# Six PSUM tiles of one bank for the products of a Strassen-like expert layer, new planner costs and a new order of work

## The chip, the core and the metric

The kernel runs as one program on one core of a Trainium2 chip. The core has five engines that run side by side, each with its own queue that is worked off strictly in order: TensorE (PE, matrix products; its weight loads are listed as PEld), VectorE (DVE), ScalarE (ACT), GpSimd (POOL) and SyncE (SP, which issues most of the DMAs). Products are summed up in PSUM, which has eight banks of 512 float32 numbers per partition. The metric is the device time of one execution in microseconds (us); lower is better.

## The reference

What is computed is an attention block whose output goes through a layer of experts. Each of 2304 tokens picks 2 of 8 experts by noisy logits; an expert is two matrix products with a ReLU between them.

```python
# attention: q, k, v are (4, 8, 576, 64)
q_rot, k_rot = rotate(q), rotate(k)
attn = softmax(q_rot @ k_rot.T / sqrt(64))
x = (attn @ v).transpose(0, 2, 1, 3).reshape(2304, 512)
# experts: w1 is (8, 512, 1024), w2 is (8, 1024, 512)
noisy = x @ w_gate + log1p(exp(x @ w_noise)) * noise
top2, top2_w = two largest of noisy per token, softmax over the two
for e in range(8):
    for k in range(2):
        mask = top2[:, k] == e
        h = maximum(x[mask] @ w1[e], 0)
        out[mask] += top2_w[mask, k, None] * (h @ w2[e])
```

## The kernel before, in words

**Two halves.** Attention and routing fill roughly the first 345 us. The tokens are written to a table in memory with room for 624 (`CAP`) tokens per expert (five tiles of 128), and the experts follow. Every float32 operand is split into a float16 high and a float16 low part, and each product is the sum of three: high by high, high by low, low by high. ACT makes the high part of a piece and DVE the low part; the pair of instructions is called a cast here.

**Experts 0 and 1** are computed plainly. `up` makes one block of 128 hidden rows for 256 or 368 tokens at a time (12 matmuls for the narrow form, each 256 or 368 columns wide), into a PSUM tile from a ring of three (`big`, two banks each); ACT (L1559) and DVE (L1557) then write its high and low part to `hid`, and only then is the tile free for the third block after it. There are 16 blocks for the first 256 tokens of both experts and 16 wide ones (368 columns) for the rest.

**Experts 2 to 7** use seven products of half-size blocks in place of eight, for the first layer (`seven`). The 624 tokens are two halves of 312, and the 1024 hidden rows are taken in two passes `p`, each with two blocks of 128 rows, `g` = 0 and 1. Sums of weight blocks are made by DVE (L1303 to L1309, cast in L1291 and L1295) and sums of token blocks by POOL (`plan_turns`, L1354 to L1366, cast in L1370 and L1374). For each `p` the products run in the order P2, P1, P7, P6, P4, P5, P3, each for g = 0 and then g = 1, six matmuls of 312 columns at a time. They are added up in three PSUM tiles, called c, a and b, of two banks each: bank 0 of a tile belongs to g = 0, bank 1 to g = 1. Partial sums that are needed twice are copied to SBUF by ACT (`keep`, L1450: k1 after P1, k7 after P7, k2 after P6), added again by DVE (`join`, L1454: j11, j21, j22), and the finished quarters of the hidden layer go through ReLU to `hid` (`hide`, L1443 on ACT and L1441 on DVE): quarter 11 from c, 21 from b, 12 from a, and 22 from the copies in SBUF. Quarters 11 and 21 are read for both g in one instruction of 2 x 312 columns.

**Second layer.** `down` adds 24 matmuls of 512 columns into a tile of one bank (`dn`, a ring of two, called a down tile here); ACT scales it (`y`, L1634) and POOL adds its rows into the output (`spread`, L1643).

**What sets the order.** Each step is entered in a plan (`Plan.add`) with an engine, a duration, the steps it depends on and the buffers that it uses. `Plan.order` runs through the plan in simulated time and always starts the ready step of lowest priority number; the numbers in `CFG["dp"]`, one for each step, are added to the priorities. The order in which the steps are started is the order in which instructions are recorded for the engines, and it is fixed from then on. At run time an instruction waits through semaphores for the instructions that it depends on, as they are found from the tiles read and written, whatever the plan thought of their time.

Of the kernel before, what the change touches and what calls it, by code (L numbers as in the profile page):

```python
# [11 lines left out]
F32 = mybir.dt.float32  # L12
# [124 lines left out]
-20 2935 3206 -1718 -2012 -889 2833 4404 813 -264 2775 -2091 3378 2520 -4200 -555 -59 3739 1239 -2425 1328 1857 541  # L137
1731 -994 378 -3900 3008 -1979 -4553 -8 -3221 328 -3171 -921 -816 -284 242 1068 974 -2451 -82 5813 -913 4682 1180 5502
450 -543 5177 1264 936 -7 4727 -2533 -1839 -56 -760 785 -612 201 -5606 2097 -1110 238 -4268 -2037 2004 315 1567 -528
5925 6561 -2693 2544 2495 6494 358 -890 1789 -5127 -1907 -6509 -930 2280 5751 182 281 2260 113 223 1663 1222 473 1956  # L140
-365 89 1384 -417 724 1974 3373 1695 -625 1015 -2456 378 -1435 -871 -1680 869 1345 2982 2910 -1823 -589 -282 -258
-1914 6672 -552 219 1369 -3333 -1232 -1554 -1533 433 -1426 5310 -255 -3444 2150 -450 497 7553 -3948 521 -556 2815
-4797 -1994 -793 -6025 -1393 2002 -687 2569 2441 -1802 4019 -102 5322 509 2546 -3466 -2707 -7485 4070 4585 7698 -1354
-4162 -6438 -3748 4554 -3147 3530 -5284 -5734 -79 -19 -5230 -2269 1762 -53 -2801 -2692 -3814 -1054 -4707 -5370 -2335
3505 -655 2289 -4886 -5778 -1651 8257 4590 -378 -1056 -3623 -1022 -3014 -1981 -3423 -1771 -3914 -4682 -5788 -3312
-1153 -2329 -5816 -352 -223 -1365 -345 2932 427 -3068 -582 -4025 -2535 -3748 -3399 -459 -1075 4383 409 2227 -848 -3669
5340 -116 711 -4565 -675 -5589 -8881 3198 -1797 964 -1008 3759 4607 1097 -2978 4367 -3493 517 -3983 2305 -2224 -956
-1166 318 12 1142 -1124 -3789 1000 -1055 -721 -2210 1771 -4136 1674 -1397 4956 -4176 -2022 -5262 -241 -5058 -6736
-1466 -1994 -3337 7334 -1092 -3646 -1784 -3296 1951 1419 2833 -3878 2373 4868 -8596 -567 -3922 -4552 -5075 797 8989
1521 5332 -836 15 1950 -2365 570 -3691 6597 -2034 -2379 1096 1521 2348 2756 2911 -1633 -54 2741 572 2650 -143 3107  # L150
-2132 989 675 -1461 -1125 -938 2322 -2330 446 -730 1427 -382 5808 -383 2478 -3307 -584 -514 244 546 365 -1138 -457
-1372 585 1203 1935 -2118 -505 -920 1547 1164 2577 3085 -3523 211 2713 1097 544 443 -527 -1831 971 -996 -167 1178 774
-1828 -3308 465 -1014 1242 -265 648 -3251 -210 -4359 -261 119 -3433 1404 -386 -1274 1400 -688 -2361 -1871 899 334 -719
-2542 -190 -340 -106 2497 803 -2006 1602 -1626 3772 631 26 158 -1600 -163 388 -2908 1324 -720 -1070 -607 -2443 295 313
902 2122 1652 -728 854 3213 -48 -737 -1898 1253 1276 -4328 640 2949 359 2667 2111 1808 2082 -1925 -427 -78 594 -2373
1834 267 -3015 -28 1233 -715 -1145 -2563 854 -2598 -1427 648 -1543 -1512 100 2308 -428 -330 -77 814 -162 -1171 2632
-3574 -791 1090 1519 -599 2349 639 -331 -540 2479 -1094 781 1653 2217 -2051 1008 250 357 829 -1702 -2453 685 1253 1426
1432 501 3575 4393 732 -2277 1345 -3405 -1987 946 1503 -3280 -1832 228 755 -334 2032 -1447 1648 862 759 909 21 -660
2838 2983 -495 470 2516 1177 -1130 -2956 151 986 -953 790 -2830 -826 1394 900 -395 1140 -787 -966 2382 4866 3434 -401
-598 -3176 1813 1453 -1127 -1193 -1650 -2271 -1503 296 2068 1291 -425 3759 -762 2649 675 807 -1079 -2599 -1816 1949  # L160
-4331 -450 -8 606 280 -519 -1564 -245 1707 -1434 -694 -749 578 663 374 640 -1041 922 -1141 -1802 -3330 -1008 -3773
-4744 -1154 -1524 1241 2212 2762 518 387 -2497 1464 635 -901 -2389 -1214 193 264 2647 -1357 227 -124 152 -2548 400
-2834 2721 -1291 1761 -235 -2002 -680 331 963 -57 1228 -14 -2481 -1216 -1043 304 2443 -4481 969 3036 2635 -1831 -1182
786 737 -3898 -1866 -3171 5090 -1390 416 89 -1897 -157 1875 1019 -1283 320 1149 -2490 1000 360 271 1068 -177 1754 2189
3976 -131 946 2000 -147 105 -3204 -2409 1026 -1540 1659 4616 291 -253 -955 -515 -3285 1284 -961 -2554 -2372 2401 -73
-3263 -910 -1325 1421 -1479 -2403 -3694 447 -669 1293 -2539 -196 -814 1651 1733 -1978 549 1025 3513 387 382 1037 -1508
-131 2169 -187 1221 -891 -1190 2149 1664 -346 -1248 569 14 156 508 1495 968 -1635 2063 3392 824 -2278 465 -850 -3234
642 -1202 1127 725 427 -2014 569 -764 739 5699 -555 2525 -520 1634 -483 3036 2228 -3023 864 2778 -566 1534 -625 -3059
3206 3154 -768 -2052 1644 535 -1343 492 4811 -2844 2570 -4654 -556 -3476 1593 -1389 -1849 -1590 679 2786 767 1269
-1981 -3289 1351 -493 -3567 -238 -799 -2346 -3957 -25 791 -3086 1442 -998 -1576 1241 978 344 -97 -9 2488 43 -1323 4897  # L170
# [1738 lines left out]
```

## Time and profile before

| | us |
|---|---|
| median of 3 runs | 763.6 |
| lowest and highest | 760.75, 763.7 |
| profiled execution | 769.25 |
| its span (first instruction to last) | 767.5 |
| PE busy in the span | 709.8 |
| DVE, POOL, ACT busy in the span | 512.2, 421.2, 365.1 |

The profiled execution is a single one, and longer than the median of the others; what lies around its span is the difference of 1.75 us. Times of instructions below are counted from the span's start. A busy PE in this table is one that has a matmul under way. A wait is told by the engine that waits and by the instruction whose end released it. The page also gives PE's granted clock, in shares of full speed (2.4 GHz; the other level is 1.2 GHz).

### The profile page before, as it was taken

The numbers are of one execution on the slowest core, as the hardware profiler recorded it, in microseconds if no ns is written. First come the engines' busy times: TensorE is split into PE (matmuls) and PEld (weight loads), VectorE is DVE, ScalarE is ACT, GpSimd is POOL, SyncE is SP. The second block draws the span as 40 slices with busy tenths as digits, with TensorE's granted clock in tenths as the row PEclk, the third lists the DMA queues.
The fourth block names the chain that finished last, engine by engine and source line by source line (L and its number), as shares of the span: only waits on it lengthen the run. The fifth ranks groups of instructions, "written<-read, shape, count | busy, mean of one in ns | idle before, by whom it ended". The sixth has DMA issues, their size and how long they took to land.

```text
span 767.5 us, 18738 instructions
## 1 busy us (share of the span) xinstructions
PE 709.8 (92%) x7988; PEld 488.3 (64%) x7988; DVE 512.2 (67%) x801; ACT 365.1 (48%) x602; POOL 421.2 (55%) x332
## 2 busy tenths in 40 slices
PE   4899998899889899889999798999999999999996
PEld 4677777788777777778555345556465565554652
DVE  5757769886859669577217658929879497594331
ACT  2543555564546664855124236637456455473310
POOL 5699798896614686835611486191460822902311
PEclk9999999999799999999999999999999999999998
DMA  6686465966517594574674462663735627514211
GB/s 157 149 138 136 115 141 116 191 139 144 115 52 159 190 212 149 162 195 169 215 201 113 97 192 34 143 187 76 207 86 126 174 56 201 137 61 97 54 66 41
DMA packets 178285, 103.50 MB, mean 135 GB/s; under 512 B 150136, under 2 KB 154744, under 8 KB 178192
## 3 DMA queue, kind: packets, MB, share of 16 engines
q1 hardware_dynamic: 161632, 72.72, 40.2%
q0 software_dynamic: 8592, 20.38, 11.4%
q10 hardware_dynamic: 7968, 9.12, 3.6%
q8 instruction: 64, 1.05, 0.6%
q14 instruction: 29, 0.24, 0.1%
HBM read 49.92 MB, written 29.22 MB: 103 GB/s over the span
## 4 chain that ended last, share of the span: by engine, by line
PE 61%; DVE 11%; ACT 7%; issue 2%; DMA 1%; SPq 0%; POOL 0%; POOLq 0%; ACTq 0%; DVEq 0%
PE ps L574 27%; PE dn L574 26%; PE acc L574 7%; DVE nm L599 1%; DVE xr L813 1%; ACT p L699 1%; DVE w1l L1295 1%; DVE hid L1441 1%; DMA qt<-tq 1%; ACT xr L815 1%; ACT ps L699 1%; ACT xr L1450 1%; ACT hid L1443 1%; ACT w1h L1291 1%; DVE w2l L1178 1%
## 5 line engine op out<-in xcount | busy, mean ns | idle before, releaser
L574 PE MATMUL dn<-w2h,hid 128*128 128x512 f16 x640 | 193.9, 380 | 0.0
L1643 POOL DMA_INDIRECT out_dram<-y,meta x40 | 67.2, 1679 | 219.2 <-ACT y L1634 186.1
L574 PEld LDWEIGHTS <-hid 128*128 128x128 f16 x960 | 94.1, 98 | 111.1 <-issue 1.3
L574 PE MATMUL dn<-w2l,hid 128*128 128x512 f16 x320 | 121.6, 380 | 0.0
L710 POOL TENSOR_TENSOR p<-p 128x1152 f16<-128x1152 f32 (+1 forms) x48 | 100.0, 2096 | 29.9 <-ACT p L699 28.2
L699 ACT ACTIVATE p<-ps,pbias 128x576 f32<-128x576 f32 x112 | 79.9, 740 | 71.7 <-PE ps L574 70.3
L599 DVE TENSOR_REDUCE nm<-ps 128x2 f32<-128x576 f32 x128 | 90.6, 749 | 25.2 <-PE ps L574 24.9
L574 PE MATMUL ps<-qt,kt 64*128 64x288 f16 (+5 forms) x1200 | 85.4, 264 | 8.7 <-DVE nm L599 3.3
L574 PE MATMUL acc<-vb,p 128*128 128x65 f16 (+3 forms) x2040 | 78.4, 194 | 8.3 <-DVE xr L813 6.9
L574 PE MATMUL ps<-xt,w1h 128*128 128x312 f16 (+2 forms) x384 | 81.0, 304 | 4.8 <-DVE hid L1557 4.0
L574 PEld LDWEIGHTS <-p 128*128 128x128 bf16 (+3 forms) x2040 | 70.7, 98 | 21.0 <-issue 16.0
L574 PEld LDWEIGHTS <-w1h 128*128 128x128 f16 x640 | 62.8, 98 | 33.1 <-issue 9.4
L574 PE MATMUL ps<-kt,qt 64*128 64x288 f16 (+1 forms) x960 | 79.8, 291 | 2.9 <-DVE nm L599 0.8
L574 PEld LDWEIGHTS <-kt 64*128 64x128 f16 (+1 forms) x1200 | 54.2, 98 | 22.8 <-issue 14.6
L1634 ACT ACTIVATE y<-dn,gsc 128x512 f32<-128x512 f32 x33 | 22.6, 685 | 88.0 <-PE dn L574 74.2
L1178 DVE SCALAR_TENSOR_TENSOR w2l<-wst,w2h 128x1024 f16<-128x1024 f32 x25 | 41.4, 1671 | 29.8 <-ACT w2h L1176 29.8
L574 PEld LDWEIGHTS <-qt 64*128 64x128 f16 (+1 forms) x960 | 46.3, 98 | 19.0 <-issue 8.7
L574 PE MATMUL ps<-xt,w1l 128*128 128x312 f16 (+2 forms) x192 | 58.3, 303 | 0.0
L1441 DVE SCALAR_TENSOR_TENSOR hid<-ps,hid 128x624 f16<-128x624 f32 (+1 forms) x48 | 30.5, 639 | 32.6 <-ACT hid L1443 32.2
L1110 POOL DMA_INDIRECT xs_rows<-xr,r_ii x36 | 37.5, 1042 | 22.8 <-DVE gsc L1514 12.9
L574 PE MATMUL ps<-qlm,cm 64*128 64x288 f16 (+5 forms) x440 | 47.0, 255 | 0.0
L1450 ACT COPY xr<-ps 128x312 f32<-128x312 f32 x72 | 28.1, 423 | 28.1 <-PE ps L574 27.6
(196 smaller groups left out, 1289.8 us busy)
## 6 DMA issues: line engine op xcount, KB each, us to landing
wst<-in_moe_w_dram SPq DMA_DIRECT2D x51, 512.0 KB, 4.0
wst_r<-in_moe_w_dram SPq DMA_DIRECT2D x13, 512.0 KB, 6.0
out_dram<-pad ACTq DMA_DIRECT2D x18, 256.0 KB, 3.7
xs_rows<-pad ACTq DMA_DIRECT2D x8, 522.0 KB, 4.5
qin<-in_q_dram SPq DMA_DIRECT2D x16, 256.0 KB, 4.6
qin<-in_k_dram SPq DMA_DIRECT2D x16, 256.0 KB, 4.0
vin<-in_v_dram SPq DMA_DIRECT2D x16, 256.0 KB, 3.4
out_dram<-y,meta POOLq DMA_INDIRECT x40, 4.9
```

Source lines behind the costliest of these rows:

```text
L574: nc.tensor.matmul(o, w, m, start=first, stop=last, skip_group_check=True)
L599: nc.vector.tensor_reduce(nm()[:, u, :, h], x, axis=AX.X, op=OP.max, negate=True)
L699: nc.scalar.activation(x if way[u] == "P" else halves(whole(u), u, h), x, AF.Exp, bias=pbias, scale=0.125 / (QS * QS))
L710: E.tensor_tensor(b, whole(u), a, op=OP.subtract)
L813: nc.vector.tensor_tensor(at_, xx, to, op=OP.subtract)
L815: nc.scalar.copy(to, xx)
L1110: i = nc.gpsimd.indirect_dma_start(out=xs, out_offset=bass.IndirectOffsetOnAxis(ap=h["ii"][:, t, a:a + 1], axis=0), in_=r[:, slot(t)], in_ ...
L1178: nc.vector.scalar_tensor_tensor(lo[:, c:c + step], h[c], sc, hi[:, c:c + step], op0=OP.mult, op1=OP.subtract)
L1441: nc.vector.scalar_tensor_tensor(s["hl"][:, f0:f0 + n, cols:cols + HALF], src_(), 0.0, h, op0=OP.max, op1=OP.subtract)
L1450: add((nm, e, p, g), "ACT", .33, lambda: nc.scalar.copy(snap(k, g), bank(r, g)), deps=[dep], uses=[b[r, g], sb[k, g]], prio=pr)
L1634: nc.scalar.activation(y, dn(), AF.Copy, scale=s["gsc"][j])
L1643: i = nc.gpsimd.indirect_dma_start(out=out, out_offset=bass.IndirectOffsetOnAxis(ap=ids(e, j, 0), axis=0), in_=yt[0], in_offset=None, boun ...
```

## The change

1. **PSUM tiles.** Where experts 2 to 7 begin (`banks`), the ring of three two-bank tiles is closed, and a pool of six tiles of one bank each takes its place, one for each of c, a, b and each g. So that this can be done, the accumulator of the attention (`sml`) and the down tiles (`acc`) are placed from the other side of PSUM. The instructions that hide quarters 11 and 21 are split in two, one for each g; the plan has 48 steps more (2654, before 2606).
2. **Costs in the plan.** Sums of tokens on POOL are planned longer, loads of an expert's tokens get another issue time and a landing time by size, and a scatter on POOL is planned with 1.7 in place of 1.07.
3. **Order.** The table `CFG["dp"]` has new numbers from the routing of the third batch on; all steps before that keep theirs.

```diff
-20 2935 3206 -1718 -2012 -889 2833 4404 813 -264 2775 -2091 3378 2520 -4200 -555 -59 3739 1239 -2425 1328 1857 541
+-20 2935 3206 -1718 -2012 -889 2833 4404 813 -264 2775 -2588 4328 2216 -2425 -1857 1073 4370 2214 -2985 943 4208 454
...
-    big = ctx.enter_context(tc.tile_pool(name="big", bufs=3, space=PSUM))
-    manual, attn, early, sums_ = ExitStack(), ExitStack(), ExitStack(), ExitStack()
+    manual, attn, early, sums_, big_ = ExitStack(), ExitStack(), ExitStack(), ExitStack(), ExitStack()
+    big = big_.enter_context(tc.tile_pool(name="big", bufs=3, space=PSUM))
-    sml = sums_.enter_context(tc.tile_pool(name="sml", bufs=1, space=PSUM))
+    sml = sums_.enter_context(tc.tile_pool(name="sml", bufs=1, space=PSUM, side="right"))
...
-        pools["acc"] = ctx.enter_context(tc.tile_pool(name="acc", bufs=2, space=PSUM, reuse_waits="tile"))
+        pools["acc"] = ctx.enter_context(tc.tile_pool(name="acc", bufs=2, space=PSUM, side="right", reuse_waits="tile"))
...
-                return .08 + m * HALF * (1.04e-3 if E == "DVE" else 2.1e-3 if m == 4 else 2.6e-3)
+                return .08 + m * HALF * (1.04e-3 if E == "DVE" else 2.3e-3 if m == 4 else 3.1e-3)
...
-    zb = []
+    zb = {}
     def banks():
-        zb.extend(big.tile([128, 1024], F32, name="ps") for _ in range(3))
+        big_.close()
+        pz = ctx.enter_context(tc.tile_pool(name="zs", bufs=1, space=PSUM, reuse_waits="tile"))
+        for a in range(3):
+            for g in range(2):
+                zb[a, g] = pz.tile([128, 512], F32, name="z%d%d" % (a, g))
...
-            return zb[role[r]][:, 512 * g:512 * g + HALF]
+            return zb[role[r], g][:, 0:HALF]
...
-        hide("11", lambda: pair("c"), g2, 2, 0, both("j11"), [b["c", 0], b["c", 1]], pos["P7"] - FIRST + 3)
-        hide("21", lambda: pair("b"), 4 + g2, 2, 0, both("j21"), [b["b", 0], b["b", 1]], pos["P4"] - FIRST + 1)
+        for g in range(2):
+            hide("11", lambda g=g: bank("c", g), g2 + g, 1, 0, [P("j11", g)], [b["c", g]], pos["P7"] - FIRST + 3 + .1 * g)
+            hide("21", lambda g=g: bank("b", g), 4 + g2 + g, 1, 0, [P("j21", g)], [b["b", g]], pos["P4"] - FIRST + 1 + .1 * g)
...
-        add(("x", e, c0), "SP", 1.1 * n + .4, f, deps=deps + ["swap_right"] + ([] if e == 0 and c0 == 0 else ["swap_left"]),
-            uses=([xbuf[0, "xt"]] if e == 1 and c0 == 0 else []) + [xbuf[e, c0], mbuf[e, c0]], prio=pr, land=1.25 * n + .2)
+        add(("x", e, c0), "SP", .8 * n + 1.4, f, deps=deps + ["swap_right"] + ([] if e == 0 and c0 == 0 else ["swap_left"]),
+            uses=([xbuf[0, "xt"]] if e == 1 and c0 == 0 else []) + [xbuf[e, c0], mbuf[e, c0]], prio=pr, land={2: 1.5, 3: .9}.get(n, .05))
...
-        add(("sp", e, j), "POOL", 1.07, spread, deps=[("y", e, j)] + ([("zero", i) for i in range(18)] if e == 0 else []) +
+        add(("sp", e, j), "POOL", 1.7, spread, deps=[("y", e, j)] + ([("zero", i) for i in range(18)] if e == 0 else []) +
```

**Place 1: VectorE at the end of the wide first-layer blocks of experts 0 and 1.** L1557 (L1562 after the change) writes the low part of such a block (`hid<-ps`, 128x368); the other rows make sums of expert 2's weights (`wst`, `sw`) and the low parts of its casts (`w1l`, `xr`). Before:

```order
L1295 SCALAR_TENSOR_TENSOR w1l_8032<-wst_r,w1h_8031 128x2x512
L1307 TENSOR_TENSOR wst<-sw,wst 128x512
L1309 TENSOR_TENSOR wst<-wst_r,wst 128x512
L1557 SCALAR_TENSOR_TENSOR hid<-ps,hid 128x368
L1295 SCALAR_TENSOR_TENSOR xr_100<-sw,xr_100 128x512
L1295 SCALAR_TENSOR_TENSOR w1l_8032<-sw,w1h_8031 128x512
L1295 SCALAR_TENSOR_TENSOR xr_100<-wst,xr_100 128x2x512
L1557 SCALAR_TENSOR_TENSOR hid<-ps,hid 128x368 x2
```

And VectorE in the same place after the change:

```order
L1562 SCALAR_TENSOR_TENSOR hid<-ps,hid 128x368 x2
L1298 SCALAR_TENSOR_TENSOR w1l_8027<-wst_r,w1h_8026 128x2x512
L1298 SCALAR_TENSOR_TENSOR w1l_8027<-wst,w1h_8026 128x2x512
L1562 SCALAR_TENSOR_TENSOR hid<-ps,hid 128x368
L1310 TENSOR_TENSOR wst<-sw,wst 128x512
L1312 TENSOR_TENSOR wst<-wst 128x512
L1306 TENSOR_TENSOR sw<-wst 128x512
L1308 TENSOR_TENSOR sw<-wst,wst_r 128x512
L1298 SCALAR_TENSOR_TENSOR xr_100<-wst,xr_100 128x2x512
L1562 SCALAR_TENSOR_TENSOR hid<-ps,hid 128x368
```

Before, all eight sums of expert 2's weights (L1303 to L1309) stand ahead of the 12th block, the first L1557 shown, and three casts more ahead of the 13th and 14th. After the change two of the sums stand ahead of the 12th block, and the other six behind the 13th, which is the row between the casts of 2x512 and the sums.

**Place 2: POOL, where the sums of expert 2's tokens begin.** The DMA rows are scatters of finished down tiles, L1354 to L1366 (L1357 to L1369) are the sums. Before:

```order
L1643 DMA out_dram<-y,meta 2304x512
L1642 MEMSET spacer 1x1
L1643 DMA out_dram<-y,meta 2304x512
L1354 TENSOR_TENSOR xr_100<-xt 128x1248
L1358 TENSOR_TENSOR xr_100<-xr_100 128x624
```

And POOL in the same place after the change:

```order
L1648 DMA out_dram<-y,meta 2304x512
L1357 TENSOR_TENSOR xr_100<-xt 128x1248
L1647 MEMSET spacer 1x1
L1648 DMA out_dram<-y,meta 2304x512
L1361 TENSOR_TENSOR xr_100<-xr_100 128x624
```

The first sum has moved ahead of the scatter of the fifth down tile.

**Place 3: ScalarE, expert 4, pass p = 0.** L1450 (L1454) are the copies `keep`, L1443 (L1447) the ReLU to `hid`, L1291 (L1294) casts of expert 5's weights. Before:

```order
L1450 COPY xr_101<-ps 128x312 x2
L1291 ACTIVATE w1h_9303<-wst 128x2x512
L1291 ACTIVATE w1h_9303<-wst 128x512
L1443 ACTIVATE hid<-ps 128x2x312
L1634 ACTIVATE y<-dn,gsc 128x512
L1450 COPY xr_101<-ps 128x312 x2
L1291 ACTIVATE left<-sw 128x512
L1443 ACTIVATE hid<-ps 128x2x312
```

And ScalarE in the same place after the change, where `z` with a number is one of the six new tiles:

```order
L1447 ACTIVATE hid<-z_8232 128x312
L1454 COPY xr_101<-z_8236 128x312
L1447 ACTIVATE hid<-z_8233 128x312
L1639 ACTIVATE y<-dn,gsc 128x512
L1454 COPY xr_101<-z_8237 128x312
L1454 COPY xr_101<-z_8234 128x312
L1454 COPY xr_101<-z_8235 128x312
L1294 ACTIVATE w1h_9293<-sw 128x512
L1447 ACTIVATE hid<-z_8236 128x312
L1447 ACTIVATE hid<-z_8237 128x312
```

The ReLU of 2 x 312 columns has become two of 312, each from its own tile, and the casts that stood ahead of the first of them have moved.

## Rows read from the trace of the kernel before

**Rows 1.** page of the profile: busy us (share of the span) xinstructions of each engine

```profile
PE 709.8 (92%) x7988; PEld 488.3 (64%) x7988; DVE 512.2 (67%) x801; ACT 365.1 (48%) x602; POOL 421.2 (55%) x332
```

**Rows 2.** busy time by stretch, us: length, PE, PEld, DVE, ACT, POOL, PEclk, DMA

```profile
343.00:420.00 77.00, 76.29 (x565) 50.60 (x566) 37.72 (x102) 27.56 (x53) 25.98 (x45) 0.98 0.60 172
420.00:437.00 17.00, 12.99 (x66) 6.74 (x64) 12.32 (x12) 2.83 (x6) 9.12 (x6) 0.90 0.36 86
...
460.00:490.00 30.00, 26.75 (x179) 17.98 (x177) 25.60 (x36) 17.66 (x33) 12.14 (x10) 0.94 0.32 68
490.00:735.00 245.00, 239.14 (x1415) 138.17 (x1414) 167.51 (x222) 123.35 (x206) 103.59 (x87) 1.00 0.50 123
735.00:768.00 33.00, 25.62 (x122) 11.62 (x119) 5.47 (x8) 0.95 (x2) 5.22 (x9) 0.92 0.11 40
```

**Rows 3.** chain of waits, 421 to 437 us: start us, us, what

```profile
420.88 0.61 DVE wst L1307
...
421.51 3.94 DVE wst L1309
...
430.40 0.46 DVE hid L1557
...
430.91 3.02 PE ps L574 x12
```

**Rows 4.** busy time by stretch around two waits: the granted clock stands behind POOL

```profile
431.00:435.40 4.40, 4.40 (x17) 2.04 (x17) 1.36 (x4) 0.48 (x1) 0.00 (x0) 0.61 0.02 2
...
472.00:476.20 4.20, 4.03 (x18) 2.45 (x18) 2.92 (x6) 1.93 (x4) 0.45 (x2) 0.59 0.03 5
```

**Rows 5.** POOL in order of time, 392 to 432 us: start, us, what [idle before]

```profile
419.85 2.47 POOL L1643 DMA_INDIRECT out_dram<-y,meta  x1 [26.30 <-ACT y L1634]
421.76 3.14 POOL L1354 TENSOR_TENSOR xr<-xt 128x1248 f32<-128x1248 f16 x1
424.97 1.85 POOL L1358 TENSOR_TENSOR xr<-xr 128x624 f32<-128x624 f32 x1
```

**Rows 6.** chain of waits, 440 to 768 us, at expert 2

```profile
439.80 2.59 PE dn L574 x12
...
458.72 3.99 PE ps L574 x30
...
468.97 2.75 DVE w1l L1295
```

**Rows 7.** who TensorE waited for, 490 to 768 us: us in total, times, longest

```profile
PE ps L574 <- DVE hid L1441: 3.4, 6, 0.8
PE ps L574 <- DVE xr L1454: 1.1, 2, 0.6
PE ps L574 <- ACT xr L1450: 1.1, 4, 0.4
```

**Rows 8.** chain of waits, 440 to 768 us, at expert 7

```profile
722.07 1.76 PE ps L574 x12
...
723.86 0.44 ACT hid L1443
...
724.32 0.49 DVE hid L1441
...
724.84 0.44 ACT hid L1443
...
725.30 0.49 DVE hid L1441
```

**Rows 9.** groups of instructions by shape: busy us, mean ns of one, idle before

```profile
L1441 DVE SCALAR_TENSOR_TENSOR hid<-ps,hid 128x624 f16<-128x624 f32 x24 | 19.2, 799 | 24.2 <-ACT hid L1443 24.2
...
L1443 ACT ACTIVATE hid<-ps 128x624 f16<-128x624 f32 x24 | 16.6, 692 | 15.1 <-DVE ps L1454 15.0
...
L1441 DVE SCALAR_TENSOR_TENSOR hid<-ps,hid 128x312 f16<-128x312 f32 x24 | 11.3, 478 | 8.3 <-ACT hid L1443 8.0
...
L1443 ACT ACTIVATE hid<-ps 128x312 f16<-128x312 f32 x24 | 10.1, 429 | 13.7 <-PE ps L574 10.0 <-DVE xr L1454 1.8 <-DVE hid L1441 1.6
```

More of the change, by code (lines that the diff above doesn't have):

```diff
@@ L1406, in bank @@
         def bank(r, g):
-            return zb[role[r]][:, 512 * g:512 * g + HALF]
-        def pair(r):
-            return zb[role[r]].rearrange("p (g n) -> p g n", g=2)[:, :, 0:HALF]
+            return zb[role[r], g][:, 0:HALF]
         def src(x, k, lo):
```

104 rows, old and new, of the table CFG are left out of this document.

## The prediction

> **What bounds the kernel now.** I read the page's busy times first: TensorE has a matmul under way for 709.8 of 767.5 us [rows 1], so nothing but TensorE's idle time, and the time that it works at the lower clock, can be won. The order of every engine is the same as before up to the routing of the third batch, at about 343 us, so I cut the rest of the span into stretches [rows 2]. From 343 to 420 us TensorE idles 77 - 76.3 = 0.7 us. From 420 to 437 it idles 17 - 13.0 = 4.0, from 460 to 490 it idles 30 - 26.75 = 3.25, from 490 to 735 it idles 245 - 239.1 = 5.9. After 735 stands the end: the last down tiles, one scale, one scatter. The last pass and the last down tiles keep their order on TensorE, and I leave this end as it is.
>
> Then I read why. At 420 to 437 us [rows 3] the reader is to see TensorE start a wide block at 430.91 us behind a row of DVE instructions, the longest of them a weight sum (L1309) of 3.94 us, where a sum of the same width just before takes 0.61. The wait costs more than its idle time: from 431.0 to 435.4 the granted clock is 0.61 [rows 4], a mean of stretches at full speed and at half of it (1.2 of 2.4 GHz), so 4.4 x 0.39 = 1.7 us of work is lost after it. TensorE had idled for most of the 5 us before; the same is seen from 472.0 to 476.2 (0.59, again 1.7 us) behind the wait at expert 2. No third such fall stands between 490 and 735, where the clock is 1.00 [rows 2].
>
> In the stretch of experts 3 to 7 the waits are short: 12 are listed, the longest 0.8 us, and six of them are for the DVE part of a ReLU (L1441) [rows 7]. One of them is written out at expert 7 [rows 8]: ACT 0.44, DVE 0.49, ACT 0.44, DVE 0.49, strictly in turn. These are two casts, of g = 0 and of g = 1, that have no data in common. ACT's part of the second waits for DVE's part of the first since both read one two-bank tile. That is the cost of the old tiles, and it is what I take the change to remove. Beyond its idle time each wait costs TensorE a refill: 12 matmuls that start after one take 1.76 us [rows 8], and 30 in stride take 3.99 [rows 6], which is 1.60 for 12, so 0.16 us.
>
> What can be won between 343 and 735 us is therefore: 4.0 + 1.7 + 2 x 0.16 = 6.0 at the wide blocks, 3.25 + 1.7 + 3 x 0.16 = 5.4 at expert 2, and 5.9 + 14 x 0.16 = 8.1 at experts 3 to 7 (14 waits, two of them too short for the list). The sum is 19.5 us.
>
> **The change, part by part.** *Order at the wide blocks (6.0 us).* A block may start when the third one before it has left its PSUM tile. Before, the 15th and 16th wait for the 12th and 13th, whose DVE parts stand behind all eight weight sums and casts behind them (place 1). After the change the 12th and 13th stand ahead of six of the sums, and only two weight casts come between them. TensorE does one more wide block before the down tiles, so it arrives at the 14th only after three half down tiles of 2.59 us [rows 6], 7.8 us later than the 13th ended, and those DVE parts of 0.5 us are long done. What is late next is the 16th block's own DVE part, now behind a token cast and two weight casts. It is needed only by expert 1's down tiles, three half tiles (7.8 us) behind the last block on TensorE. The first token sum on POOL moves ahead of a scatter (place 2). In the trace POOL idled 26.3 us behind that scatter until ACT had scaled a down tile [rows 5]; the sum needs only the tokens, but their load is issued when expert 0's last wide block is through, and that moves little, so the sum still runs at about 420 to 423 us, and the rest of the sums a scatter later. So DVE still meets POOL there, and I allow it the whole 3.14 + 1.85 us of [rows 5] as delay: 5 us, less than the 7.8. I count all 6.0; the bounds are 0 and 6.0.
>
> A rule of the Trainium skill bears on this place. The row shows 3.94 us in place of 0.61 for a DVE sum that began 0.25 us before a POOL sum of 3.14, and it ended 0.55 us after the POOL sum did [rows 3, 5]. The page "SBUF — State Buffer" (section "Who interferes with whom") says that a DVE instruction with two inputs in SBUF and a GpSimd instruction that reads SBUF hold a port pair in turn, each for its whole length. By it 3.9 us is POOL's sum and then DVE's own 0.6, which the trace agrees with; by a mere slowing, DVE would lose less for shorter sums.
>
> *One-bank tiles at expert 2 (5.4 us).* Two waits here are not of the old tiles: before, DVE makes a weight cast (L1295) of 2.75 us [rows 6] beside POOL's token sums, and j22 stands behind it. The new order puts j22 ahead of such a cast, but expert 3's eight token sums now stand nearly in one piece on POOL, beside the same products; DVE was busy for 25.6 of 30 us [rows 2] before. I count half, 2.7 us: the tiles give every product of g = 0 one more product of slack on each side. Bounds: all 5.4 gone, or 3 us worse with another fall of the clock (1.7).
>
> *One-bank tiles at experts 3 to 7 (8.1 us).* A product of 6 matmuls takes 0.80 us (3.99 for 30 [rows 6]). Before, k7 of g = 0 waits until P7 of g = 1 is done, and P4 of g = 0 waits until k7 of g = 1 is done, and so for k1, k2 and j22. With a tile for each g both go: 0.8 us of slack on either side, 1.6 together, against waits of at most 0.8 [rows 7]. The exceptions are casts that stand ahead of a copy on ACT, which are another order. I count 6.6 of the 8.1 as gone; bounds 3 and 8.1.
>
> *Split of the hides.* 24 instructions of 624 columns on each of DVE and ACT (799 and 692 ns) become 48 of 312 (478 and 429 ns) [rows 9]: DVE gets 24 x (2 x 0.478 - 0.799) = 3.8 us more, ACT 24 x (2 x 0.429 - 0.692) = 4.0. DVE has 167.5 of 245 us in the last stretch [rows 2], so this lies beside TensorE; if it didn't, it would cost 0.16 at each of 24 places. But the first half starts before the second join is made, so a bank comes free earlier: 0. The new pool itself waits for tiles that are long read: 0, at most one wait of 0.5.
>
> *New costs and the rest of the order.* The costs change nothing but the order. A new order has waits that the old trace can't show: I take 1.7 us, one wait as short as those of [rows 7] (5.6 us for 12, so 0.47 and a refill) in about every second of the 12 passes of half an expert, less what is counted above; bounds 0 and 7 (every pass).
>
> Sum: 6.0 + 2.7 + 6.6 - 1.7 = 13.6 us. The profiled execution took 769.25, 1.75 more than its span; it would take 755.6. The median of the runs is 763.6, 5.65 lower, and the same 13.6 from it gives 750.0 us.
>
> **The rivals.** *POOL takes back what the tiles give.* The token sums for experts 3 to 7 stand more in one piece, and each DVE sum or cast that meets one waits for its end. At expert 2 nothing would be won and 3 us lost (5.7 less than my sum), and at experts 3 to 6 it would cost about 1 us each: 13.6 - 5.7 - 4 = 4 us, 759.6. For it: the 3.94 us [rows 3]; against it: the joins and hides read PSUM and have one input in SBUF, and the mean of a hide of 312 is 478 ns [rows 9] in a stretch with all of the sums. By the Trainium skill's rule named above the delay per meeting is the whole rest of the POOL instruction, which is the price used here.
>
> *The waits are backlog and not tiles.* If ACT and DVE come late because casts stand ahead of the copies, slack of 1.6 us is used up by a cast of 1 to 2 us, and only the wide blocks' 6.0 us goes, less 1.7: 4.3 us, 759.3. For it: four of 12 waits are for ACT copies [rows 7]. Against it: the sequence of [rows 8] holds no cast. If the new tiles were still waited for as a pair, the same sum would come out.
>
> *Slower: the tokens' sums come late at each expert.* P7 needs the summed tokens. On POOL they stand behind scatters, each of which waits for ACT's scale of a down tile (26.3 us of idle [rows 5]). If the new order lets a scatter hold them so that P7 waits, it does so at experts 2 to 7, six times. From 13.6 / 6 = 2.3 us a time the kernel is slower than before; at 4 us, with half of a clock fall (0.9), it is 6 x 4.9 - 13.6 = 16 us slower, 779. For it: scatters and sums are mixed anew; against it: no wait of TensorE for a token cast (L1374) is in the lists of before, and the sums are planned longer now, so earlier.
>
> **How the numbers follow.** Chances: my forecast 0.62, with a range of its own from 744 to 756; POOL 0.15; backlog 0.14; slower 0.07; the rest, 0.02, is no change. A measurement of this kernel tells 0.5% (3.8 us) from no change, so faster means under 759.8. The two rivals near 759.5 fall on either side of it: I put 0.20 of their 0.29 with faster, since each could also win a little more than its sum, and 0.09 with no change. Faster: 0.62 + 0.20 = 0.82; same: 0.09 + 0.02 = 0.11; slower: 0.07. If all 19.5 us go the time is 744.1; with both rivals' middle it is 759.6. The range from 744.0 to 759.8 leaves out the slower case, no change, and the slow half of the two rivals.
>
> **What would show it.** In the profile after: between 420 and 437 us no idle time of TensorE over 0.5 us and a granted clock of 1.00; the idle time in the products of experts 3 to 7 in sum below 1.5 us, with no ACT hide of g = 1 released by a DVE hide of g = 0; L1447 and L1445 at 312 columns with means near 429 and 478 ns. If expert 2's products still wait over 2 us for a DVE join behind a cast, POOL's sums are what I sized wrong. If TensorE's waits for joins and copies stay as many as before with the same lengths, the tiles were not the cause. If TensorE waits for L1377, the slower rival has come.

## The result, and the profile after

| | before | after |
|---|---|---|
| median, us | 762.17 (4 runs) | 753.23 (4 runs) |
| lowest and highest | 760.7, 763.7 | 751.14, 754.91 |
| profiled execution | 769.25 | 751.14 |

The ratio is 0.9881 with a 95% interval from 0.9839 to 0.9923: faster by 8.9 us, or 1.2%. The first line of the page after answers to [rows 1]: TensorE is busy 9.6 us less, DVE 11.2 us more. Of these, 24 x (2 x 0.474 - 0.799) = 3.6 are the split ReLUs (shapes below); the rest comes with the new order, since with the same tiles in the order before (E10 below) DVE is busy for 509.1 us in all.

```profile
PE 700.2 (93%) x7988; PEld 482.7 (64%) x7988; DVE 523.4 (70%) x825; ACT 370.0 (49%) x626; POOL 418.8 (56%) x332
```

Not all of the 18 us between the two profiled executions is the change. Up to the third batch's routing, where the order on every engine is the same, the execution before took 7.9 us longer, in part at a lower granted clock (0.86 in place of 0.97 from 200 to 250 us). So I count from there on: from the first transposes of that batch on TensorE (339.59 us before, 331.67 after) to the end of the last down tile it is 421.0 and 410.8 us, 10.2 less.

The stretches that answer to [rows 2] (length, PE, PEld, DVE, ACT, POOL, PEclk, DMA): the wide blocks of expert 1, expert 2, the down tiles of expert 2 with expert 3's products, and all that follows up to the last down tiles.

```profile
409.00:430.00 21.00, 21.00 (x109) 10.48 (x107) 17.66 (x18) 7.95 (x13) 13.12 (x9) 1.00 0.73 165
447.00:471.00 24.00, 22.16 (x165) 15.93 (x164) 21.70 (x34) 16.03 (x33) 14.29 (x11) 1.00 0.23 53
471.00:524.00 53.00, 49.27 (x284) 28.16 (x283) 37.60 (x53) 25.54 (x47) 21.50 (x18) 0.97 0.48 114
524.00:733.00 209.00, 209.00 (x1229) 120.20 (x1228) 150.45 (x199) 103.83 (x184) 83.09 (x73) 1.00 0.48 121
```

TensorE has no idle time left at the wide blocks (4.0 us before) and none from 524 to 733 us, where 209.00 of 209 us are busy. It still idles 1.8 us at expert 2, and 3.7 us at expert 3, where the waits before the change were 0.4 us at most. Who it waited for from 343 us on (us in total, times, longest), answering to [rows 7]:

```profile
PE z L577 <- ACT xr L1454: 2.8, 1, 2.8
PE z L577 <- DVE hid L1445: 1.8, 3, 0.8
PE z L577 <- DVE xr L1458: 0.9, 1, 0.9
PE ps L577 <- DVE r_sel L1067: 0.5, 1, 0.5
PE ps L577 <- DVE nf L1669: 0.3, 1, 0.3
```

Of the 12 waits of [rows 7] none is left from expert 4 on. How the false ones went can be read at expert 7, where [rows 8] had ACT and DVE strictly in turn. Here are the two ReLUs of quarter 12, first on ACT, then on DVE, each in order of time (start, us, what, [idle before <- who ended it]):

```profile
706.27 0.43 ACT L1447 ACTIVATE hid<-z 128x312 f16<-128x312 f32 x1 [1.11 <-PE z L577]
707.07 0.43 ACT L1447 ACTIVATE hid<-z 128x312 f16<-128x312 f32 x1 [0.36 <-PE z L577]
```

```profile
706.74 0.48 DVE L1445 SCALAR_TENSOR_TENSOR hid<-z,hid 128x312 f16<-128x312 f32 x1 [0.73 <-ACT hid L1447]
707.53 0.48 DVE L1445 SCALAR_TENSOR_TENSOR hid<-z,hid 128x312 f16<-128x312 f32 x1 [0.31 <-ACT hid L1447]
```

ACT's second ReLU (707.07) is released by TensorE, not by DVE's first (706.74 to 707.22), and runs beside it. The shapes that answer to [rows 9] (busy us, mean ns of one, idle before):

```profile
L1445 DVE SCALAR_TENSOR_TENSOR hid<-z,hid 128x312 f16<-128x312 f32 x72 | 33.0, 474 | 26.4 <-ACT hid L1447 26.3
...
L1447 ACT ACTIVATE hid<-z 128x312 f16<-128x312 f32 x72 | 29.9, 429 | 25.4 <-DVE z L1458 17.4 <-PE z L577 7.4
```

Now the place that lost. The chain of waits from 480 to 513 us (start, us, what):

```profile
482.10 11.46 DMA xt<-xs_rows
...
493.70 0.03 POOL xr L1357
...
496.43 6.39 DMA out_dram<-y,meta
...
502.93 0.69 ACT y L1639
...
504.45 0.64 ACT xr L1454 x2
...
505.13 3.28 PE z L577 x12
...
509.31 1.99 DVE w1l L1298
...
512.52 0.56 PE z L577 x3
```

Read it from the end. TensorE (505.13, the product P4 of expert 3, p = 0) waits for the copies k7 on ACT. These stand behind `y`, the scale of expert 2's fifth down tile (502.93). The buffer of `y` is free when a scatter has landed (496.43 + 6.39). The scatter stood on POOL behind a token sum that waited until 493.70 for expert 4's tokens. For 3.3 us after the wait the granted clock is 0.52, near half speed, a loss of 3.3 x 0.48 = 1.6 us (same columns as above):

```profile
505.10:508.40 3.30, 3.27 (x14) 1.92 (x14) 3.30 (x2) 0.62 (x2) 3.30 (x3) 0.52 0.28 39
```

A second cause offers itself on ACT, ahead of the same copies: a weight cast that waits 2.80 us for its load.

```profile
497.55 1.06 ACT L1294 ACTIVATE w1h<-wst 128x1024 f16<-128x1024 f32 x1 [2.80 <-DMA wst<-in_moe_w_dram]
...
502.93 0.69 ACT L1639 ACTIVATE y<-dn,gsc 128x512 f32<-128x512 f32 x1 [2.96 <-DMA out_dram<-y,meta]
```

That load, too, stands behind the tokens, on SP (start, us in which SP is held, what):

```profile
482.10 9.39 SPq L1509 DMA_TRANSPOSE xt<-xs_rows  x1
...
492.16 1.46 SPq L1268 DMA_DIRECT2D wst<-in_moe_w_dram  x3
```

The tokens go into a ring of two buffers. Expert 2's P3 (p = 1, g = 1) is the last to read the older one. Before the change it stood ahead of expert 2's first down tile; now it stands behind the second, 10.4 us after the first began. The load was issued at the first down tile's start before (487.27 us, and held SP for 4.84 us); after it is issued 11.4 us behind that start (482.10 against 470.70) and holds SP for 9.39.

### The profile page after: what moved, and what is told of

The parts are those of the page before. It is cut to its first block, busy times and chain, and to the rows that moved or that the text cites. A ratio compares the mean times of both kernels' runs of the same rounds, so it can differ in the third digit from the quotient of the medians.

```text
span 749.4 us, 18781 instructions
## 1 busy us (share of the span) xinstructions
PE 700.2 (93%) x7988; PEld 482.7 (64%) x7988; DVE 523.4 (70%) x825; ACT 370.0 (49%) x626; POOL 418.8 (56%) x332
## 4 chain that ended last, share of the span: by engine, by line
PE 57%; DVE 9%; DMA 5%; ACT 5%; issue 3%; POOL 2%; SPq 1%; POOLq 0%; ACTq 0%; DVEq 0%
PE dn L577 21%; PE z L577 15%; PE ps L577 13%; PE acc L577 7%; DMA out_dram<-y,meta 3%; DMA xt<-xs_rows 2%; DVE nm L602 1%; ACT p L702 1%; DVE xr L816 1%; ACT ps L702 1%; ACT xr L818 1%; ACT p L706 1%; POOL out_dram L1648 1%; DVE w2l L1181 1%; DVE acc L797 1%
## 5 line engine op out<-in xcount | busy, mean ns | idle before, releaser
L1445 DVE SCALAR_TENSOR_TENSOR hid<-z,hid 128x312 f16<-128x312 f32 x72 | 33.0, 474 | 26.4 <-ACT hid L1447 26.3
L1357 POOL TENSOR_TENSOR xr<-xt 128x1248 f32<-128x1248 f16 x7 | 21.6, 3092 | 37.9 <-DMA xt<-xs_rows 37.9
L1447 ACT ACTIVATE hid<-z 128x312 f16<-128x312 f32 x72 | 29.9, 429 | 25.4 <-DVE z L1458 17.4
L577 PE MATMUL z<-xr,w1h 128*128 128x312 f16 x192 | 39.8, 303 | 2.8 <-ACT xr L1454 2.8
```

What stands on the lines that cost most here:

```text
L577: nc.tensor.matmul(o, w, m, start=first, stop=last, skip_group_check=True)
L1357: eng_of(CFG['sum']['x']).tensor_tensor(x.rearrange("p (a b) n -> p a (b n)", a=2), xt[:, i:4:2, 0:CAP], xt[:, 4 + i:8:2, 0:CAP], op=OP.add)
L1445: nc.vector.scalar_tensor_tensor(s["hl"][:, f0:f0 + n, cols:cols + HALF], src_(), 0.0, h, op0=OP.max, op1=OP.subtract)
L1447: nc.scalar.activation(h, src_(), AF.Relu)
```

## The experiments

Theories at the start: **A**, the tiles end false waits from expert 2 on; against it **B**, the new order does. **E**, the 2.8 us at expert 3 come from the late token load, through POOL; against it **F**, they come from the late weight load. Theories C, D, G and H are told in the expectations. E1 to E4 ran on one chip, E5 to E8 on a second, E9 to E12 on a third, each kernel in five rounds with the kernel before beside it. Where steps are moved, this edit is made, with a list of moves for each kernel: of each pair, the step named first is put right ahead of the second on its engine, and all other steps keep their order there:

```diff
-    todo = plan.order()
+    todo = shift(plan.order())
```

**E1, the changed kernel again.**

> The changed kernel once more, unedited, so that the edits below have it beside them on the same chip. Every theory: 753 us, 9 us less than the kernel before, and the same waits of TensorE: 2.8 us for an ACT copy at expert 3, pass 0 (505 us), 0.9 us for a DVE join soon after, 1.8 us in three waits at expert 2, none over 0.5 us from expert 4 on. If the 2.8 us are gone here, they were an accident of one execution.

Measured: 765.09 us against 783.06, ratio 0.9775 (0.9743 to 0.9807). The waits are those expected (4.1, 1.0, 2.0 us), but on this chip all kernels are longer. Compared with the first trace of the same kernel, 8.3 us are lost between the third batch's routing and expert 0's third down tile. In the middle of it TensorE worked 9.07 of 15 us (14.80 in the same place of the first trace). Its longest wait there, 4.2 us, was for a ReLU on ACT, and ACT had waited 4.6 us, and then 1.8, for something that the trace can't name:

```profile
362.00:377.00 15.00, 9.07 (x57) 5.54 (x56) 4.21 (x11) 1.43 (x4) 8.45 (x16) 0.92 0.52 196
```

In E3, with the order of before, the same stretch is 13.0 us longer than in the trace before. So the times of E1 to E4 are compared with each other only, and what is said of stretches leaves this one out.

**E2, two-bank tiles in the new order.**

```diff
-            for g in range(2):
-                zb[a, g] = pz.tile([128, 512], F32, name="z%d%d" % (a, g))
+            zb[a] = pz.tile([128, 1024], F32, name="z%d" % a)
...
-            return zb[role[r], g][:, 0:HALF]
+            return zb[role[r]][:, 512 * g:512 * g + HALF]
```

> The changed kernel with its order, costs and split ReLUs, but with three PSUM tiles of two banks again. Theory A (the tiles end the waits from expert 3 on): the waits of g = 0 for copies and ReLUs of g = 1 come back at experts 2 to 7, 12 or more of them, mostly for DVE ReLUs, 5 to 8 us with refills; the wide blocks of experts 0 and 1 keep their gain. 753 + 7 = 760 us (757 to 762). Rival B (the new order ends them): 753 us, and no more waits at experts 4 to 7 than in the changed kernel. Rival C (the split ReLUs end them, since each half starts earlier): 753 us too, so A is told from B and C.

Measured: 775.91 us, 10.8 more than E1; ratio 0.9911 (0.9879 to 0.9944). TensorE's waits from expert 2 on:

```profile
PE z L577 <- ACT xr L1453: 5.8, 4, 4.2
PE z L577 <- DVE hid L1444: 3.7, 7, 1.0
PE z L577 <- DVE xr L1457: 3.6, 7, 1.0
```

These are 18 waits in place of 5, ten of them at experts 4 to 7, where E1 has none: A holds, B and C fall. The price is above what I had expected (7); by the traces 6.5 us are lost at experts 4 to 7 and 2.9 at experts 2 and 3.

**E3, the tiles alone.** Before with `banks` as changed, and both halves of a paired ReLU recorded one behind the other:

```diff
-            return zb[role[r]].rearrange("p (g n) -> p g n", g=2)[:, :, 0:HALF]
+            return [bank(r, g) for g in range(2)]
...
-                h = s["hh"][:, f0:f0 + n, cols:cols + HALF]
+                z = src_()
+                for f, m, z in [(f0 + g, 1, z[g]) for g in range(2)] if isinstance(z, list) else [(f0, n, z)]:
+                    h = s["hh"][:, f:f + m, cols:cols + HALF]
```

> The kernel before with its own order and costs, but with six PSUM tiles of one bank; a step that hid both g in one instruction now records two, one behind the other. Theory A (tiles): the waits of experts 3 to 7 fall from 8.1 us (5.9 and refills) to under 2, expert 2 loses about 2 of its 5.4, the wide blocks of experts 0 and 1 keep theirs (3.9 us idle and a fall of the clock): 762.2 - 8 = 754 us (752 to 757). Rival B (order): 762 us, the waits as before. Rival D (casts stand ahead of the copies, backlog): the list of waits shrinks by less than half, 759 us.

Measured: 771.31 us, 11.8 less than before; ratio 0.9858 (0.9823 to 0.9892). E10 repeats it where nothing disturbs the first stretch.

**E4, expert 4's tokens loaded early.**

```diff
+MOVES = [
+    (('P3', 2, 1, 1), ('dn', 2, 0, 0)),
+    (('x', 4, 0), ('w', 3, 'w2', 3)),
+]
```

> The changed kernel with two steps moved: P3 of expert 2 (p = 1, g = 1) ahead of expert 2's first down tile on TensorE, as before the change, and the load of expert 4's tokens ahead of a load of expert 3's weights on SP. Theory E (the tokens' buffer comes free 10 us late, POOL waits 9.9 us for the load, the scatters behind it and the scale on ACT are late, and the copies behind the scale hold TensorE): POOL's wait of 9.9 us shrinks by 8 us or more, the 2.8 us wait of TensorE at expert 3 goes, with it the fall of the clock behind it (1.7 us) and the 0.9 us wait: 753 - 5 = 748 us (747 to 749.5). Rival F (the ACT copies are late because a weight cast on ACT waits 2.8 us for its own load, which now stands no earlier on SP): the wait stays at 2 us or more, 752 to 754 us. Rival G (the meeting of DVE with POOL's token sums sets it): it moves with the sums, and a wait of like size turns up elsewhere: 752 to 754 us.

Measured: 760.18 us, 4.9 less than E1; ratio 0.971 (0.9679 to 0.9741). The load now holds SP for half as long as in the first trace, and the wait for k7 is gone:

```profile
483.91 4.69 SPq L1509 DMA_TRANSPOSE xt<-xs_rows  x1
```

One wait at expert 3 is left, grown from 1.0 us (E1) to 1.7; here is why, first DVE, then POOL:

```profile
513.76 4.11 DVE L1298 SCALAR_TENSOR_TENSOR w1l<-sw,w1h 128x512 f16<-128x512 f32 x1
517.79 1.99 DVE L1298 SCALAR_TENSOR_TENSOR w1l<-wst,w1h 128x512 f16<-128x512 f32 x1
519.70 0.87 DVE L1458 TENSOR_TENSOR z<-z,xr 128x312 f32<-128x312 f32 x2
520.48 0.85 DVE L1458 TENSOR_TENSOR xr<-z,xr 128x312 f32<-128x312 f32 x2
```

```profile
513.40 1.41 POOL L1369 TENSOR_TENSOR xr<-xr 128x312 f32<-128x312 f32 x1
514.21 3.10 POOL L1357 TENSOR_TENSOR left<-xt 128x1248 f32<-128x1248 f16 x1
517.38 1.84 POOL L1361 TENSOR_TENSOR left<-left 128x624 f32<-128x624 f32 x1
519.31 1.17 POOL L1365 TENSOR_TENSOR left<-left 128x312 f32<-128x312 f32 x1
```

A weight cast that takes 0.68 us elsewhere takes 4.11, and ends 0.56 us after POOL's sum of 3.10; the next takes 1.99 and ends 0.56 after the sum of 1.84. The joins behind them (0.87 for two, one operand in PSUM) run beside a third sum without loss. So the big wait comes from the late tokens, and the small one from what G names. E4 doesn't decide by which path the tokens act: with the move the weight load of F (L1268) is issued earlier too, 9.6 us after expert 2's first down tile began, against 21.5 in the first trace. E5 takes this up.

The rule for the small wait is the one that the prediction named, of the Trainium skill ("SBUF — State Buffer", section "Who interferes with whom"): a DVE instruction with two inputs in SBUF and a GpSimd instruction that reads SBUF contend for a port pair, which one of them holds for its whole length. The trace agrees in the length of the delays and in that the joins are spared. What the rows leave open is the turn: the first cast began while a shorter sum (L1369) was on POOL, 0.45 us before the sum of 3.10, and still had to wait for both.

**E5, the scatters ahead of the late sum.**

```diff
+    (('sp', 2, 2), ('t', 4, 0, 0)),
+    (('sp', 2, 3), ('t', 4, 0, 0)),
```

> The changed kernel with one move: on POOL the scatters of expert 2's third and fourth down tile stand ahead of the first sum of expert 4's tokens; the load of these tokens stays late. Theory E (late tokens hold the scatters, these the scale on ACT, this the copies k7 that TensorE waits for): the scatters run when their tiles are scaled, the scale of the fifth tile waits for no scatter, and TensorE's wait of 2.8 to 4.1 us for an ACT copy at expert 3 goes with the fall of the clock behind it: 4 to 6 us less than the changed kernel, though x(4) is loaded as late as there. Rival F (ACT's copies are late because the weight cast on ACT waits for its load): the wait stays over 2 us. If E is right and the sums, now later still, make new waits, they show as waits of DVE or TensorE for POOL's sums behind 510 us.

Measured: 753.25 us against 764.51, ratio 0.9874 (0.9829 to 0.9919). The changed kernel itself has 0.9881 in the result and 0.988 in E12, on other chips. `y` waits for no scatter now, but TensorE still waits 3.5 us for the copies (506.88). ACT:

```profile
501.32 1.06 ACT L1294 ACTIVATE w1h<-wst 128x1024 f16<-128x1024 f32 x1 [4.74 <-DMA wst<-in_moe_w_dram]
504.11 0.63 ACT L1294 ACTIVATE xr<-sw 128x512 f16<-128x512 f32 x1 [1.74 <-DVE sw L1306]
...
505.48 0.68 ACT L1639 ACTIVATE y<-dn,gsc 128x512 f32<-128x512 f32 x1
...
506.88 1.39 ACT L1454 COPY xr<-z 128x312 f32<-128x312 f32 x4
```

Theory E as I had written it, one chain over POOL, is too narrow. With that link cut, the same late load reaches ACT by the weight cast behind it (4.74 us, rival F) and by a DVE sum (1.74 us) that stands behind a DVE step waiting for the tokens' `meta`. (The load held SP for 10.68 us in this execution, so that what stands behind it came later still; but the ratio over all runs is no better either.) The earlier load of E4 moved all three paths. E4 made that load both earlier and shorter on SP, and no run tells the two apart.

**E6, only the split of the ReLUs:** the edit shown at E3 in the kernel before, with its two-bank tiles.

> The kernel before with its order and its three tiles of two banks; only the ReLUs of 2 x 312 columns are split in two of 312. Forecast's step (the split costs nothing and, without the tiles, brings nothing): the kernel before within 2 us. Rival H (the 3.8 us more on DVE lie on the path): 3 to 5 us slower. Rival C (the split itself is what ends the waits): 6 us or more faster.

Measured: 765.61 us against 764.51, ratio 1.0004 (0.9977 to 1.003). No cost and no gain; the waits from expert 2 on stay:

```profile
PE ps L574 <- DVE hid L1443: 3.9, 7, 0.8
PE ps L574 <- DVE xr L1456: 3.9, 6, 2.0
PE ps L574 <- ACT xr L1452: 2.2, 5, 0.9
```

**E7, tiles and four moved steps,** in the order before.

```diff
+    (('hl', 1, 4, 256), ('w', 2, 'w1', 0, 's4')),
+    (('hl', 1, 6, 256), ('w', 2, 'w1', 1, 's4')),
+    (('hh', 1, 6, 256), ('w', 2, 'w1', 1, 'e', 'h')),
+    (('hh', 1, 1, 256), ('w', 2, 'w1', 1, 'e', 'h')),
```

> The kernel before with its order and costs, six tiles of one bank (as in the run of the tiles alone), and four steps moved at the wide blocks: the DVE ReLUs of the 12th and 13th block ahead of the weight sums s4, and the ACT ReLUs of the 13th and 14th ahead of the cast that waits for the second s4. Theory (the whole gain there is DVE's order): TensorE's waits of 1.1 and 2.9 us and the fall of the clock go, 6 us less than with the tiles alone, 17 to 18 us less than the kernel before on a chip where the tiles alone win 11.8, or 14 to 15 on one where the changed kernel wins 9. Rival (the later position of the blocks on TensorE is needed too): a wait of 1 us or more stays for an L1563, and 3 us or less are won.

Measured: 748.22 us, 16.3 less; ratio 0.9777 (0.974 to 0.9815). TensorE has no wait at the wide blocks. On DVE the ReLUs of the 12th and 13th block now stand ahead of the sum (L1309) that took 3.94 us in [rows 3]:

```profile
414.12 0.53 DVE L1563 SCALAR_TENSOR_TENSOR hid<-ps,hid 128x368 f16<-128x368 f32 x1
...
420.96 0.54 DVE L1563 SCALAR_TENSOR_TENSOR hid<-ps,hid 128x368 f16<-128x368 f32 x1 [1.62 <-ACT hid L1565]
421.42 1.90 DVE L1309 TENSOR_TENSOR wst<-wst_r,wst 128x512 f32<-128x512 f32 x1
```

**E8, early load and casts late,** in the changed kernel: E4's two moves and ten of casts and sums, of which these are the two at expert 3 and the first at expert 2:

```diff
+    (('w', 4, 'w1', 0, 'c', 'l'), ('hl', 3, 5, 1, '21')),
+    (('w', 4, 'w1', 0, 'a', 'l'), ('hl', 3, 5, 1, '21')),
+    (('w', 3, 'w1', 0, 's2'), ('w', 3, 'w1', 1, 'a', 'l')),
```

> The changed kernel with the two moves of the early load, and 10 moves of weight casts and sums on DVE and ACT: at expert 2, sums s2 and s4 and four casts of expert 3's weights behind the ReLUs and joins that TensorE waits for; at expert 3, two casts of expert 4's weights behind the joins j21 and j22. Theory (what is left of waits at experts 2 and 3 is DVE held in casts and sums of weights by POOL's token sums, 0.7 us turned into 2 to 4): the three waits at expert 2 (1.9 us) and the one at expert 3 (1.7 us) go, 4 us less than with the early load alone. Rival (DVE has too much to do there, and the work only meets the next product): waits of the same sum turn up at other products of experts 2 and 3, 0 to 1 us won.

Measured: 749.59 us, 14.9 less than before; ratio 0.9806 (0.9775 to 0.9838). Expert 2's three waits and expert 3's are gone, and one of 0.8 us has come at expert 3's next pass:

```profile
PE z L577 <- DVE hid L1445: 0.8, 1, 0.8
```

By the traces it is 2.4 us better at expert 2 and 0.8 at expert 3 than E4, 3.2 of the 4 expected; the rival had a fifth of the truth. The medians show less: the changed kernel wins 8.2 to 8.9 us where nothing disturbs it and E4 another 4.9, which is 13.1 to 13.8, so 14.9 is 1.1 to 1.8 us more. The traced execution (745.8 us) is the fastest of E8's six.

**E9, four moved steps alone,** E7's list in the kernel before, with two-bank tiles.

> The kernel before with its three tiles of two banks and its order, and only the four steps moved at the wide blocks. Theory (the gain there is DVE's order and needs neither tiles nor the new order on TensorE): the waits of 1.1 and 2.9 us and the fall of the clock behind them go, 6 us less than the kernel before, 755 to 758 where that takes 762 to 764; every wait from expert 2 on stays. Rival (the time won comes back at expert 2, whose weight sums and casts are made later now): 0 to 3 us less, with longer waits at expert 2.

Measured: 758.4 us against 764.71, ratio 0.992 (0.9891 to 0.9949). That is 6.3 us less, with every wait from expert 2 on left as it was and one of 0.4 us more at expert 2. There, TensorE's wait of 2.0 us for j22 is the one of [rows 4], but no fall of the clock stands behind it, where the trace before had 0.59 (columns as in [rows 2]):

```profile
461.10:465.30 4.20, 3.60 (x26) 2.53 (x26) 3.93 (x8) 2.94 (x5) 0.46 (x2) 1.00 0.04 6
```

**E10, the tiles alone again.**

> The six tiles alone in the order before, once more, beside the others on one chip. By the traces so far the tiles are worth 10 to 11 us from expert 2 on, whatever the chip: 752 to 754 us where the kernel before takes 763. If the 11.8 us measured first had a part in what is lost at 363 to 376 us on that chip, it is less here, 5 to 8 us.

Measured: 753.86 us, 10.9 less than before; ratio 0.985 (0.9813 to 0.9888). From 400 us on TensorE waits at the wide blocks and hardly anywhere else:

```profile
PE ps L574 <- DVE hid L1563: 4.0, 2, 2.9
PE z L574 <- ACT xr L1456: 0.5, 1, 0.5
PE z L574 <- DVE xr L1460: 0.3, 1, 0.3
PE z L574 <- DVE hid L1447: 0.3, 1, 0.3
```

**E11, a better version:** E7 and five more moves.

```diff
+    (('w', 1, 'w2', 0, 'l'), ('hl', 1, 1, 0)),
+    (('w', 3, 'w1', 0, 'd', 'h'), ('w', 3, 'w1', 0, 'a', 'h')),
+    (('w', 3, 'w1', 0, 'd', 'l'), ('w', 3, 'w1', 0, 's2')),
+    (('hl', 2, 4, 2, '22'), ('w', 3, 'w1', 0, 's2')),
+    (('w', 7, 'w1', 1, 'a', 'l'), ('w', 7, 'w1', 0, 'c', 'l')),
```

> The order before, six tiles, the four steps moved at the wide blocks, and five more: a weight cast on DVE behind a ReLU at the narrow blocks; on ACT and DVE the cast of S3 (expert 3) behind a copy, and with the ReLU of quarter 22 behind those of quarter 12, at expert 2; a weight cast behind two joins at expert 6. Theory (each of TensorE's last waits from 345 us on, 0.6, 0.5, 0.3 and 0.3 us, is a cast that stands ahead of what TensorE waits for): they go, with a refill of 0.16 each, 2 us less than without these five, 16 to 18 us less than the kernel before: about 746. Rival (the waits only pass to the next instruction): same as without the five, 748.

Measured: 746.13 us, 18.6 less than before and 10.4 less than E12; ratio 0.9751 (0.972 to 0.9782). It beats both kernels. All of TensorE's waits that the view lists from 343 us on:

```profile
PE z L574 <- DVE xr L1460: 0.2, 1, 0.2
```

**E12, the changed kernel beside them.**

> The changed kernel beside the three others: 9 to 10 us less than the kernel before on a chip where that takes 763, so about 7 us more than the version with the order before, six tiles and nine moved steps.

Measured: 756.49 us, 8.2 less than before; ratio 0.988 (0.9846 to 0.9914). The waits for k7 (3.2 us) and at expert 2 (2.0) are there again. The 0.9 us wait at expert 3 isn't: it comes and goes with the execution.

## Why the prediction was right, and where it was not

The table is worked out from the traces: the time between the starts of two fixed instructions on TensorE, less the same time in the trace before, and less the work that an order moves across the boundary (1.87 us for a wide block, 0.80 for a product). For one and the same order such differences repeat within 0.1 us at the wide blocks and at experts 4 to 7 and within 0.5 at expert 3. At expert 2 they repeat within 0.2, but for the trace before itself.

| us, from routing of the third batch | after | E12 | E9 moves | E10 tiles | E7 both | E8 | E11 |
|---|---|---|---|---|---|---|---|
| narrow blocks | +1.5 | +1.5 | 0.0 | -0.3 | -0.2 | +0.5 | -1.0 |
| wide blocks | -6.0 | -6.0 | -6.0 | 0.0 | -6.0 | -6.0 | -6.0 |
| expert 2 | -3.1 | -2.9 | -1.1 | -4.1 | -4.1 | -5.4 | -5.0 |
| expert 3 | +4.1 | +4.6 | 0.0 | -1.6 | -1.6 | -0.4 | -1.6 |
| experts 4 to 7 | -6.7 | -6.7 | 0.0 | -6.0 | -6.0 | -6.7 | -6.5 |
| sum | -10.2 | -9.5 | -7.1 | -12.1 | -18.0 | -18.1 | -20.2 |
| by medians | -8.9 | -8.2 | -6.3 | -10.9 | -16.3 | -14.9 | -18.6 |

(E9 keeps before's order at expert 2, and is 1.1 us shorter there. That much of the trace before is its own, a fall of the clock that not every execution has; every kernel's expert 2 is set against it, so each sum is some 1 us too good. The medians are lower by 0.8 to 1.7 us, but for E8.)

- *Wide blocks, 6.0 us:* measured 6.0. E9 shows that four steps on DVE and ACT do it, without tiles and without a change on TensorE; the later arrival of TensorE, which I had put first, isn't needed.
- *Expert 2, 2.7 of 5.4 us:* measured 3.1, but only 2.0 against an execution like E9's. The 1.7 us that I had put for a fall of the clock came from one execution; E9 has the wait without it. So the agreement is partly luck. The rest stayed for the reason given, DVE's weight sums and casts beside POOL's token sums, only that TensorE now waits for ReLUs behind them and not for j22. With them moved behind what TensorE needs (E8), the whole 5.4 goes by the traces.
- *Experts 3 to 7, 6.6 of 8.1 us:* at experts 4 to 7 every wait went, 6.7 us; the tiles alone win 7.6 at experts 3 to 7 (E10). The mechanism is that of [rows 8]: E2 takes the tiles away and loses 10.8 us, and E6 shows that the split alone does nothing. That two banks need no waiting for each other agrees with a rule of the Trainium skill ("PSUM — Partial Sum Buffer", section "PSUM bank collisions raise a hardware error"): guard PSUM by bank and quadrant. Experts 4 to 7 after show readers of two banks side by side; what a collision does no run here shows.
- *Split, 0:* measured 0 (E6), within some 2 us; the means of a half in the changed kernel are 474 and 429 ns.
- ***A new order's own waits, 1.7 us:* this is the step that failed.** It measured 7.2, a little over my upper bound (7): 1.5 at the narrow blocks, and at expert 3 the 4.1 lost and the 1.6 that the tiles win there. I had spread half-microsecond waits over twelve passes; the 5.7 us at expert 3 were one chain, a wait of 2.8 us with a fall of the clock and a 0.9 us wait behind it. My sign for experts 3 to 7, less than 1.5 us of idle time, was missed there (3.7). The new order, which I had at hand, showed it: P3 of expert 2 behind two down tiles. I followed what the moved products wait for, and not which buffer they free last and which queue that holds. The 1.5 us at the narrow blocks, with short waits for routing steps on DVE (L1067 and L1669 in the list above), I had not priced at all, and no run here takes them apart.

So the sum was 13.6 and the trace gave 10.2, the medians 8.9. The time is inside the forecast's own range, for reasons that hold but for that term; that it stayed there although this term was 5.5 us short is luck in part, since the tiles won 1.7 us more than I had counted at experts 3 to 7. As for the rivals: "backlog" is excluded by E2 and E10. "POOL takes back" was real at two places, for 2.3 us at expert 2 and 0.9 at expert 3, not the 9.7 it was priced at. "Slower: tokens late" came closest to what happened: tokens were late, at one expert out of six, and there the price (5.7 us) was above the 4.9 I had put; but TensorE waited for copies behind them, not for the token casts. The remaining part of the new order is thus a loss: tiles (10.9) and four moves (6.3) come to 17.2 apart and 16.3 together, and the change made 8.9 of it. The planner's new costs act only through the order and weren't tried by themselves.

## What to carry to other kernels

Give each half of a product that is read at its own time a PSUM tile of its own: waits are found by tile, so a reader of one bank can wait for the reader of the other, as in [rows 8]. With the tiles alone (E10) one of the 12 waits of [rows 7] is left. When a new order is read, follow the buffers as well as the results: who reads a ring's oldest buffer last, which load that frees, and what stands behind that load on its queue and behind its users on POOL, DVE and ACT. And try a change's parts alone: the tiles in the old order with nine moved steps (E11) beat the new table of 2654 numbers (E12) by 10 us.

## What was not expected of the hardware

- The load of expert 4's tokens, a transposing DMA of the same size each time, held SP for 9.29 to 10.68 us in five traces (after, E1, E2, E5 and E12), for 4.69 to 5.40 in eight, and for 6.97 in E8. In the five long cases two weight loads were issued in the 2.1 us ahead of it. In the eight short ones it was one at most, 1.4 us ahead or more, and in E8 one, 0.5 us ahead. Whether these loads are the cause wasn't tried; it stays open.
- On the chip of E1 to E4, ACT and DVE stood still for 4.6 us, and then for 1.8, between 362 and 377 us (E1), with no wait that the trace names on ACT; TensorE stood behind them for 4.2. The traces from the two other chips don't show it. Its cause is open too.
